# An attention-and-gate kernel on one core: small tiled matmuls made full-array, and the start-up reordered

## The chip, the cores and the metric

The kernel runs on one core of a Trainium2 chip. The metric is device time in microseconds (us), lower is better; "before" means the kernel as it was, "the change" or "after" the changed one. The profile's span runs from the first to the last instruction of one profiled execution and is 1 to 2 us shorter than the measured time. Engines: PE is TensorE, PEld its weight loads, DVE is VectorE, ACT is ScalarE, POOL is GpSimd, SP only issues DMAs here. Every run has a state (fast or slow); only fast runs are compared, and where a profile fell in the slow state the text says so.

## The reference

Eight batches, eight heads, 576 positions, head size 64. Attention is approximated with 32 landmarks, the means of 18 positions each:

```python
q_lm = q.reshape(B, H, 32, 18, D).mean(axis=3);  k_lm = ...      # landmarks
A, Bm, C = sm(q, k_lm), sm(q_lm, k_lm), sm(q_lm, k)              # softmax of scaled products
Z = Bm^T / (norm1(Bm) * norminf(Bm))
for _ in range(6): Z = 2*Z - Z @ Bm @ Z                          # Newton, 32 x 32 per head
x = A @ Z @ C @ v
# then the gate, on x laid out as (batch, 576, 512)
proj = x @ w_proj;  x1, x2, x3 = split(proj)
y = x1 * irfft(rfft(x2) * rfft(filter)) * x3                     # over the 576 positions
out = y @ w_out
```

## The kernel before

Each batch has an attention part and a gate part. The gate of batch b is interleaved ("woven"), step by step, with the second half of the attention of b+1 and the first half of b+2. Each engine runs its own list of instructions in order, so a step that waits on TensorE's list holds up all steps behind it (in the changed kernel below TensorE stands 6.7 us for one turned K, with other work behind it in its list). FFTs are matmuls with tables of cosines and sines. Scores need K and Q with the head dimension on partitions; K and Q are loaded in natural layout by GpSimd's queue and *turned*: batch 0 by TensorE, batches 1 to 7 by a DMA transpose on SP's queue. SP's queue also carries the output stores.

```python
    def load(b, by_dma=True, with_v=True):
        kn = io.tile([R, H, NC, D], BF16, tag="kn", name="kn")      # two buffers
        qn = io.tile([R, H, NC, D], BF16, tag="qn", name="qn")
        nc.gpsimd.dma_start(kn..., k[b]...)
        nc.gpsimd.dma_start(qn..., q[b]...)
        if with_v: load_v(b)
        if by_dma:                                                   # the DMA turns
            for src, dst in ((kn, kTbufs[b % 2]), (qn, qTbufs[b % 2])):
                nc.sync.dma_start_transpose(dst[:, 0:NB, :], src...)
    ...
        def newton(last):                       # 32 x 32 tiles, 8 heads as 2 x 4
            for g in range(2):
                for a in range(4):
                    o = slice(32 * a, 32 * a + 32)
                    mm(pn[o, 1, g, :], i32[o], RZ[o, 1, g, :], start=True, stop=False)
                for a in range(4):
                    o = slice(32 * a, 32 * a + 32)
                    mm(pn[o, lo:2, g, :], RZ[o, 0, g, :], RZ[o, lo:2, g, :], start=False, stop=True)
    ...
        def scores(T, e, x, t):                 # one burst; six of them in a batch
            for h in range(H):
                for o in (0, 64):
                    mm(pc[:, o // 64, sl * m:(sl + 1) * m], Tf[o:o + 64, lo:lo + P], lm[o:o + 64, t, h, :])
            nc.scalar.activation(e[:, 2 * x:2 * x + 2, :], pc[:R, :, 0:256], AF.Exp, ...)
    ...
    # main
    tables_fwd(kc, nrow); tables_inv(sc, kb)
    for s in att[0][0] + att[0][1]: s()         # attention of batch 0
    load(1); ...; filter_spectrum(); load(2)
    for s in att[1][0]: s()                     # first half of batch 1, before gate 0
    for b in range(B):
        if b + 3 < B: load(b + 3, with_v=False)
        side = att[b + 1][1] + [load_v(b + 3)] + att[b + 2][0]      # (shortened)
        _weave(gate(b, res[b]), side)
```

The softmax here doesn't subtract the row's maximum and nothing guards it: scores larger than these inputs give would overflow.

Of the kernel before, what the change touches and what calls it, by code (L numbers as in the profile page):

```python
# [15 lines left out]
PI = math.pi  # L16
# [17 lines left out]
def kernel(  # L34
# [22 lines left out]
    FW = 2 * P + 3 * QR  # L57
# [29 lines left out]
    loaded = {}  # L87
# [6 lines left out]
    def load(b, by_dma=True, with_v=True):  # L94
        kn = io.tile([R, H, NC, D], BF16, tag="kn", name="kn")
        qn = io.tile([R, H, NC, D], BF16, tag="qn", name="qn")
        vn = vbufs[b % NV]
        nc.gpsimd.dma_start(kn.rearrange("p h c d -> p h (c d)"),
                            k[b].rearrange("h (p c) d -> p h (c d)", c=NC))
        nc.gpsimd.dma_start(qn.rearrange("p h (e c) d -> p (h e) (c d)", e=2),  # L100
                            q[b].rearrange("h (e p c) d -> p (h e) (c d)", e=2, c=3))
        if with_v:
            load_v(b)
        if by_dma:
            for src, dst in ((kn, kTbufs[b % 2]), (qn, qTbufs[b % 2])):
                nc.sync.dma_start_transpose(dst[:, 0:NB, :],
                                            src.rearrange("p h c d -> p (h c d)"))
        loaded[b] = (kn, qn, vn)

    load(0, by_dma=False)  # L110
    wproj = consts.tile([P, 4, 3 * Dm], BF16, name="wproj")
    wsrc = moe_w_proj.rearrange("(c p) j -> p c j", p=P)
    for jb in (1, 0, 2):
        nc.gpsimd.dma_start(wproj[:, :, Dm * jb:Dm * (jb + 1)],
                            wsrc[:, :, Dm * jb:Dm * (jb + 1)])
        if jb == 1:
            filt = big.tile([R, 2, 3, Dm], BF16, tag="G", name="filt")
            nc.gpsimd.dma_start(
                filt.rearrange("p e c j -> p e (c j)"),
                moe_filter_fft.rearrange("(e p c) j -> p e (c j)", e=2, c=3))  # L120
# [6 lines left out]

    poolk = consts.tile([R, m], BF16, name="poolk")
# [11 lines left out]
    nc.vector.tensor_copy(identh, ident)  # L140
    dup = consts.tile([P, 2, D], F16, name="dup")
# [25 lines left out]
    def attention(b, res, first=False):  # L167
# [3 lines left out]
        def begin():  # L171
            kn, qn, vn = loaded.pop(b)
            st.update(kn=kn, qn=qn, vn=vn, pl=wtile())
# [48 lines left out]
        def landmarks():  # L222
# [6 lines left out]
            for par in range(2):  # L229
# [3 lines left out]
            nc.vector.tensor_scalar(lm.rearrange("p t h l -> p (t h l)"), pl3,  # L233
                                    1.0 / blk, None, op0=ALU.mult)
# [3 lines left out]
        def b_scores():  # L238
# [19 lines left out]
            st.update(Bn=Bn, BT=BT)  # L258

        def b_residual():  # L260
            Bn, BT = st["Bn"], st["BT"]
            psC = stile()
            mm(psC[:, 64:128], blk4.rearrange("p a l -> p (a l)"),
               Bn.rearrange("p g l -> p (g l)"))
            for g in range(2):
                for a in range(4):
                    o = slice(32 * a, 32 * a + 32)
                    mm(psC[o, 32 * g:32 * g + 32], BT[o, g, :], BT[o, g, :])
            cm = sm.tile([P, 2], F32, tag="cm", name="cm")
            nc.vector.tensor_reduce(cm, psC[:, 64:128].rearrange("p (g l) -> p g l", g=2),  # L270
# [3 lines left out]
            RZ = sm.tile([P, 2, 2, m], F16, tag="RZ", name="RZ", bufs=3)  # L274
            for g in range(2):
                nc.vector.scalar_tensor_tensor(
                    RZ[:, 0, g, :], in0=psC[:, 32 * g:32 * g + 32],
                    scalar=cm[:, g:g + 1], in1=i32, op0=ALU.mult, op1=ALU.add)
            nc.vector.scalar_tensor_tensor(
                RZ[:, 1], in0=Bn, scalar=-1.0,  # L280
# [3 lines left out]
        steps.append(b_scores)  # L284

        def newton(last):

            RZ = st["RZ"]
            pn = stile()[:, 0:128].rearrange("p (t g l) -> p t g l", t=2, g=2)
            lo = 1 if last else 0  # L290
            for g in range(2):
                for a in range(4):
                    o = slice(32 * a, 32 * a + 32)
                    mm(pn[o, 1, g, :], i32[o], RZ[o, 1, g, :], start=True, stop=False)
                for a in range(4):
                    o = slice(32 * a, 32 * a + 32)
                    mm(pn[o, lo:2, g, :], RZ[o, 0, g, :], RZ[o, lo:2, g, :],
                       start=False, stop=True)
            if last:
                Zb = sm.tile([P, 2, 4, m], F16, tag="Zb", name="Zb")  # L300
                nc.vector.tensor_tensor(
                    Zb, pn[:, 1].unsqueeze(2).to_broadcast([P, 2, 4, m]),
                    blk4.unsqueeze(1).to_broadcast([P, 2, 4, m]), op=ALU.mult)
                st["Zb"] = Zb
            else:
                nx = sm.tile([P, 2, 2, m], F16, tag="RZ", name="RZ", bufs=3)
                nc.scalar.copy(nx, pn)  # L307
                st["RZ"] = nx

        def scores(T, e, x, t):  # L310
            pc = wtile()
            lm = st["lm"]
            Tf = T.rearrange("p x r -> p (x r)")
            for h in range(H):
                g = h // 4
                sl = 4 * g + ((h % 4) ^ g)
                lo = (3 * h + x) * R
                for o in (0, 64):
                    mm(pc[:, o // 64, sl * m:(sl + 1) * m],
                       Tf[o:o + 64, lo:lo + P], lm[o:o + 64, t, h, :])  # L320
            nc.scalar.activation(e[:, 2 * x:2 * x + 2, :], pc[:R, :, 0:256],  # L321
                                 AF.Exp, bias=0.0, scale=scale)

        def c_scores(x):
            if x == 0:
                st["eC"] = big.tile([R, NC, 256], BF16, tag="eC", name="eC", bufs=1)
            scores(kTbufs[b % 2], st["eC"], x, 1)

        def a_scores(x):
            if x == 0:  # L330
                st["eA"] = big.tile([R, NC, 256], BF16, tag="eA", name="eA", bufs=1)
            scores(qTbufs[b % 2], st["eA"], x, 0)

        steps.append(lambda: c_scores(0))
        steps.append(b_residual)
        steps.append(lambda: c_scores(1))
        steps.append(lambda: newton(False))
        steps.append(lambda: c_scores(2))
        steps.append(lambda: newton(False))
        steps.append(lambda: a_scores(0))  # L340
        steps.append(lambda: newton(False))
        steps.append(lambda: a_scores(1))
        steps.append(lambda: newton(False))
        steps.append(lambda: a_scores(2))
        steps.append(lambda: newton(False))

        def cv():
# [3 lines left out]
            for g in range(2):  # L351
                for c in range(NC):
                    for a in range(4):
# [11 lines left out]
            Cv = sm.tile([P, 2, D], BF16, tag="Cv", name="Cv")  # L365
            nc.vector.tensor_tensor(Cv, p3[:, :, 0:D],
                                    rC.unsqueeze(2).to_broadcast([P, 2, D]),
                                    op=ALU.mult)
# [22 lines left out]
        def zcv():  # L391
            pz = stile()
            for g in range(2):
                for o in (0, 64):
                    mm(pz[o:o + 64, 128 * g:128 * g + 128], st["Cv"][:, g, :],
                       st["Zb"][:, g].rearrange("p a l -> p (a l)"))
# [28 lines left out]
    INV = consts.tile([P, 5, HS], F16, name="INV")  # L425
    HH = consts.tile([P, 2, 2, 2, Dm], BF16, name="HH")
    HE = consts.tile([P, 2, 256], BF16, name="HE")
    wk = consts.tile([P, 1], F32, name="wk")
    half_pi = consts.tile([P, 1], F32, name="half_pi")
    lohi = consts.tile([P, 2], F32, name="lohi")  # L430
    TS = 2.0 * PI / S * (1.0 - 1e-7)

    def iota(t, pattern, base, cm):
        nc.gpsimd.iota(t, pattern=pattern, base=base, channel_multiplier=cm,
                       allow_small_or_imprecise_dtypes=True)
# [20 lines left out]
    def tables_iota():  # L456
        nc.vector.memset(half_pi, PI / 2)
        kc = consts.tile([R, 2 * Q + 1], F32, name="kc")
        iota(kc[:, 0:2 * Q].rearrange("p (e r) -> p e r", e=2), [[1, 2], [2, Q]], 0, 0)
        nc.vector.memset(kc[:, 2 * Q:2 * Q + 1], float(HS))  # L460
        nrow = consts.tile([R, 3], F32, name="nrow")
        iota(nrow, [[1, 3]], 0, 3)
        sc = consts.tile([P, HS], F32, name="sc")
        iota(sc, [[1, 3], [3, R]], 0, 0)


        kb = consts.tile([P, 3], F32, name="kb")
        iota(kb[:, 0:2], [[1, 2]], 0, 2)
        iota(kb[:, 2:3], [[0, 1]], 0, 1)
        return kc, nrow, sc, kb  # L470

    def tables_fwd(kc, nrow):
# [7 lines left out]
        for src, fn, tt in ((w, cosine, 0), (t, minus_sine, 1)):  # L480
            s4 = src[:, :, 0:2 * Q].rearrange("p c (e r) -> p c e r", e=2)
            for c in range(3):
                fn(F[:, c, :, P * tt:P * tt + P], s4[:, c, :, 0:P])
            lo = 2 * P + QR * tt
            for c in range(3):
                fn(F[:, c, :, lo:lo + QR], s4[:, c, :, P:Q])
        cosine(F[:, :, 0, P:P + 1], w[:, :, 2 * Q:n])
        nc.gpsimd.tensor_copy(F[:, :, :, 2 * P + 2 * QR:FW],
                              F[:, :, :, 2 * P:2 * P + QR])

    def tables_inv(sc, kb):


        x = consts.tile([P, 4], F32, name="xr")
        for a in range(4):
            o = slice(32 * a, 32 * a + 32)
            nc.vector.tensor_scalar(x[o, 0:1], kb[o, 2:3], -32.0 * a, None, op0=ALU.add)
            nc.vector.memset(x[o, 2:3], 256.0 + a % 2)
        nc.vector.tensor_scalar(lohi[:, 1:2], x[:, 0:1], 16.0, None, op0=ALU.is_ge)
# [11 lines left out]
                                op0=ALU.mult)  # L511
        nc.vector.memset(wk, 2.0 / S)
# [11 lines left out]
        sine(INV[:, 4, :], t[:, 2, :])  # L524
# [6 lines left out]
    def filter_spectrum():  # L531
        fs = big.tile([R, 2, 3, Dm], F16, tag="Y", name="fs")
        nc.vector.tensor_tensor(fs[:, 0], filt[:, 0], filt[:, 1], op=ALU.add)
# [201 lines left out]
    for s in att[1][0]:  # L735
        s()
# [41 lines left out]
```

## Time and profile before

The start of the first forward matmul of a batch's gate (`w<-F,AE` in the timeline) is used as that batch's mark throughout. A *stretch* is the time from one mark to the next; in the steady state it is the *period*.

| | before |
|---|---|
| measured, median | 274.07 us |
| first mark, second mark | 55.7, 88.7 us |
| period | 26.89 us |
| last two stretches (gate 6, gate 7 to the end) | 18.4, 30.5 us |

From the page of the kernel before, the forty-slice lines of TensorE, its granted clock and the DMA engines; each digit is a slice of 6.8 us, in tenths:

```profile
PE   0401569789999899989998999999998999998880
...
PEclk9999999999999999999999999999999999999997
DMA  6999999999999999689998997990240024006005
```

TensorE is busy from the seventh slice on, and the DMA engines are nearly full for the first 27 slices, that is 184 us. From the list of waits, the first 56 us (who waited for whom, total us, times, longest):

```profile
DVE fs L533 <- DMA filt<-in_moe_filter_fft_dram: 16.9, 1, 16.9
...
PE s L203 <- DVE kT_74 L207: 14.9, 1, 14.9
```

VectorE stood 16.9 us for the filter's load, because the filter sums came first in its list; TensorE's turn of batch 0 then stood 14.9 us for a VectorE copy behind them. The stretches of the kernel before (columns: from and to, length, busy us and count of PE, PEld, DVE, ACT, POOL, granted clock, DMA share, GB/s):

```profile
0.00:55.70 55.70, 25.57 (x572) 16.89 (x572) 26.56 (x93) 22.03 (x45) 18.04 (x47) 1.00 1.27 175
55.70:88.70 33.00, 31.39 (x549) 17.43 (x544) 20.68 (x49) 20.00 (x38) 2.52 (x3) 1.00 1.43 156
88.70:115.60 26.90, 25.82 (x476) 15.01 (x464) 19.56 (x44) 18.50 (x35) 2.51 (x3) 1.00 1.07 175
```

The trace's clock records begin only at 66.9 us, and where there is none the profile shows 1.00.

TensorE is busy 25.8 of 26.9 us in a period, but matmuls are pipelined (one of 288 columns is drawn as some 290 ns long, and the next starts 122 ns after it), so this overstates it. Start-to-start times say more: in a steady run a matmul of 288 columns follows the last one after 122 ns, one of 512 columns after 216 ns. The Trainium skill, page "TensorE: Matmul & The Clock Gate", section "Back-to-back issue gap", gives columns / 2.4 + 2.5 ns as the gap of a single matmul on the warm array, 122.5 and 215.8, and the trace agrees; the shorter gap that it gives for a sustained stream, some 131 ns at 512 columns, does not show here: 80 such gaps in four periods have a median of 216 ns, and none is under 215. Whatever a start-to-start time has above that (by over 30 ns) is called a pause here. A period then has 20.3 us of streaming, 3.9 us in 41 pauses whose releaser is "issue", and 2.7 us of waits for other engines. Where those 95 ns pauses stand is seen in the timeline of PE, merged, columns start, length, instruction:

```profile
158.29 0.34 PE L77 MATMUL w<-lm,kT_77 64*128 64x32 bf16 x13
158.56 0.30 PE L77 MATMUL w<-INV,Y 128*128 128x288 f16 x1
158.79 0.22 PE L77 MATMUL s<-BT 32*32 32x32 f16 x8
158.94 0.54 PE L77 MATMUL w<-INV,Y 128*128 128x288 f16 x3
```

One 288-column matmul starts at 158.56 and the next burst, of 32 by 32 tiles, at 158.79: 230 ns, of which 122 are streaming.

### The profile page before, as it was taken

To read this page: it belongs to the slowest core of one execution; us is meant where nothing else is said; L and a number is where in the kernel's file an instruction comes from. 1 tells how busy PE (TensorE), PEld (TensorE's weight loads), DVE (VectorE), ACT (ScalarE), POOL (GpSimd) and SP (SyncE) were. 2 spreads that over 40 slices of the span, in tenths; PEclk is the share of its full clock that TensorE was granted. 3 is DMA by queue.
4 is the path that set the end of the run, shared out by engine and by line. 5 is a ranking of instruction groups with operands and counts; after the bars stand their busy time and mean duration, and the time that the engine had idled before them with its cause. 6 is when DMAs were issued, how large, how long until landed. Compare 5 with 4: busy or idle time off the path is not lost.

```text
span 272.3 us, 8683 instructions
## 1 busy us (share of the span) xinstructions
PE 224.8 (83%) x3796; PEld 127.5 (47%) x3796; DVE 173.9 (64%) x417; ACT 161.0 (59%) x288; POOL 28.9 (11%) x60
## 2 busy tenths in 40 slices
PE   0401569789999899989998999999998999998880
PEld 0401435444654466446644664566445544633430
DVE  1029766482883878388838883798379838952950
ACT  1102974465665676667766776676667668539530
POOL 8910201201200120012001200100000000000000
PEclk9999999999999999999999999999999999999997
DMA  6999999999999999689998997990240024006005
GB/s 86 199 209 202 194 172 157 175 154 155 181 128 163 201 185 202 117 179 140 138 160 158 215 143 117 181 127 2 59 120 2 2 64 116 0 0 176 0 4 171
DMA packets 66422, 35.10 MB, mean 129 GB/s; under 512 B 46736, under 2 KB 62096, under 8 KB 66384
## 3 DMA queue, kind: packets, MB, share of 16 engines
q0 software_dynamic: 27280, 16.84, 48.3%
q1 hardware_dynamic: 39104, 17.70, 38.1%
q8 instruction: 29, 0.48, 0.8%
q14 instruction: 9, 0.07, 0.1%
HBM read 33.69 MB, written 9.44 MB: 158 GB/s over the span
## 4 chain that ended last, share of the span: by engine, by line
PE 56%; DVE 18%; ACT 13%; DMA 5%; issue 4%; POOL 1%; ACTq 0%; DVEq 0%; POOLq 0%
PE w L77 45%; PE s L77 9%; DMA filt<-in_moe_filter_fft_dram 5%; ACT X L607 4%; DVE rA L377 3%; PE s L414 2%; DVE T L609 2%; DVE gt L646 2%; DVE lm L233 1%; ACT G L598 1%; ACT eA L321 1%; ACT os L680 1%; DVE Y L611 1%; DVE rA L380 1%; DVE t L442 1%
## 5 line engine op out<-in xcount | busy, mean ns | idle before, releaser
L77 PE MATMUL w<-AT,G 128*128 128x288 f16 x256 | 41.0, 286 | 0.8 <-ACT x_5470 L644 0.4
L609 DVE TENSOR_TENSOR T<-X,HH 128x2048 bf16<-128x2048 bf16 x16 | 19.6, 1224 | 22.9 <-ACT X L607 22.9
L77 PE MATMUL w<-wout,y 128*128 128x512 bf16 x128 | 32.8, 381 | 0.4 <-DVE y L667 0.2
L377 DVE TENSOR_REDUCE rA<-eA 96x48 f32<-96x1536 bf16 x8 | 14.0, 1749 | 26.8 <-ACT eA L321 26.8
L77 PEld LDWEIGHTS <-G 128*128 128x128 bf16 x256 | 22.2, 97 | 11.3 <-issue 3.8
L598 ACT CAST G<-w 128x1024 bf16<-128x1024 f32 x24 | 24.5, 1020 | 3.6 <-PE w L77 3.6
L680 ACT COPY os<-w 128x1024 f32<-128x1024 f32 x16 | 16.2, 1012 | 16.5 <-PE w L77 16.4
L77 PE MATMUL w<-INV,Y 128*128 128x288 f16 x128 | 22.5, 288 | 0.4 <-ACT x_5443 L644 0.3
L77 PEld LDWEIGHTS <-y 128*128 128x128 bf16 (+1 forms) x192 | 13.8, 101 | 18.5 <-DVE y L667 5.4
L203 PE MATMUL s<-ident,kn 96*128 96x96 bf16 x24 | 2.4, 276 | 22.9 <-DVE kT_74 L207 14.9
L663 ACT COPY uo<-w 128x288 f32<-128x288 f32 x32 | 12.8, 399 | 13.1 <-PE w L77 9.4
L77 PE MATMUL w<-F,AE 96*128 96x304 f16 x96 | 18.9, 315 | 0.3 <-ACT os L680 0.3
L77 PE MATMUL w<-G,Ah 128*128 128x512 bf16 x64 | 18.2, 394 | 1.2 <-ACT G L598 0.5
L664 DVE TENSOR_TENSOR cv<-w,uo 128x288 bf16<-128x288 f32 x32 | 14.6, 455 | 6.7 <-ACT uo L663 6.0
L607 ACT CAST X<-w 128x1024 bf16<-128x1024 f32 x16 | 16.2, 1015 | 3.5 <-PE w L77 3.5
L587 ACT CAST Ah<-w 128x608 f16<-128x608 f32 x16 | 10.7, 671 | 11.3 <-PE w L77 11.3
L321 ACT ACTIVATE eA<-w 96x512 bf16<-96x512 f32 x24 | 13.9, 594 | 5.0 <-PE w L77 4.8
L321 ACT ACTIVATE eC<-w 96x512 bf16<-96x512 f32 x24 | 13.8, 593 | 3.8 <-PE w L77 3.1
L667 DVE TENSOR_TENSOR y<-cv,gt 128x576 bf16<-128x576 bf16 x32 | 14.5, 454 | 0.5
L665 DVE TENSOR_TENSOR cv<-w,uo 128x288 bf16<-128x288 f32 x32 | 14.3, 447 | 0.0
L307 ACT CAST RZ<-s 128x128 f16<-128x128 f32 x40 | 10.6, 266 | 5.9 <-PE s L77 5.2
L224 ACT CAST lmp<-w 128x768 f16<-128x768 f32 x8 | 6.5, 810 | 11.8 <-PE w L77 11.8
(236 smaller groups left out, 428.0 us busy)
## 6 DMA issues: line engine op xcount, KB each, us to landing
kn<-in_k_dram POOLq DMA_DIRECT2D x8, 576.0 KB, 11.5
qn<-in_q_dram POOLq DMA_DIRECT2D x8, 576.0 KB, 14.8
out_dram<-os SPq DMA_DIRECT2D x24, 192.0 KB, 3.0
vb_73<-in_v_dram POOLq DMA_DIRECT2D x4, 576.0 KB, 9.6
vb_76<-in_v_dram POOLq DMA_DIRECT2D x4, 576.0 KB, 9.2
out_dram<-os SPq DMA_DIRECT2D x16, 128.0 KB, 2.4
wproj<-in_moe_w_proj_dram POOLq DMA_DIRECT2D x3, 512.0 KB, 15.9
out_dram<-os SPq DMA_DIRECT2D x24, 64.0 KB, 2.5
```

Of the source, the lines that this page charges most:

```text
L77: nc.tensor.matmul(out_, lhsT, rhs, start=start, stop=stop, skip_group_check=True)
L321: nc.scalar.activation(e[:, 2 * x:2 * x + 2, :], pc[:R, :, 0:256], AF.Exp, bias=0.0, scale=scale)
L377: nc.vector.tensor_reduce(rA, eA.rearrange("p c (h l) -> p (c h) l", l=m), axis=AX.X, op=ALU.add)
L587: nc.scalar.copy(st["Ah"][:, g], pf[:, :, 0:FW])
L598: nc.scalar.copy(st["G"][:, :, Dm * jb:Dm * (jb + 1)], pg)
L607: nc.scalar.copy(X, px)
L609: nc.vector.tensor_tensor(T, X.unsqueeze(2).to_broadcast([P, 2, 2, Dm]), HH[:, f], op=ALU.mult)
L663: nc.scalar.copy(uo, pi[:, 1, 0:HS])
L664: nc.vector.tensor_tensor(cv_[:, 0, :], pi[:, 0, 0:HS], uo, op=ALU.add)
L665: nc.vector.tensor_tensor(cv_[:, 1, :], pi[:, 0, 0:HS], uo, op=ALU.subtract)
L667: nc.vector.tensor_tensor(st["y"][:, j, :].rearrange("p (e s) -> p e s", e=2), cv_, st.pop(f"gt{j}"), op=ALU.mult)
L680: nc.scalar.copy(os, po)
```

## The change

Its intent: (1) Newton, the residual before it, ZCv and the rest frequencies of the FFT as matmuls over the full 128 by 128 array, with block-diagonal operands, so that TensorE changes its tiling less often; (2) scores in three bursts instead of six; (3) the index tables ahead of the loads, the filter sums behind batch 0's landmarks, batch 1's first half woven into gate 0 instead of standing before it; (4) the loads of batch 2 held until batch 1 is turned. The diff, cut to its core:

```diff
+    load_k(0)                       # after the first iotas, not before everything
...
     def load_k(b):
         kn = io.tile(...)
+        ins = nc.gpsimd.dma_start(kn..., k[b]...)
+        if b == 2:
+            tc.add_manual_dep(ins.ins, after[1].ins.name, DependencyInfo(Sync, DATA))
...
+    def turn_kq(b):
+        for src, dst in zip(loaded[b], (kTbufs[b % 2], qTbufs[b % 2])):
+            after[b] = nc.sync.dma_start_transpose(dst[:, 0:NB, :], src...)
...
+            BTd = sm.tile([P, 2, 4, m], F16, ...)      # B transposed, block-diagonal
+            nc.vector.tensor_tensor(BTd, BT..., blk4..., op=ALU.mult)
...
         def newton(last):
-            pn = stile()[:, 0:128]...
+            pn = stile()[:, 0:320].rearrange("p (g x) -> p g x", g=2)
+            mm(pn[:, :, P:160], identh, RZ[:, :, P:160], start=True, stop=False)
             for g in range(2):
-                ... 16 matmuls of 32 x 32 tiles
+                mm(pn[:, g, lo:160], RZ[:, g, 0:P], RZ[:, g, lo:160], start=False)
...
+        steps.append(c_scores)          # two slots of K in one burst, one wide exp
+        steps.append(b_residual)
+        steps.append(lambda: newton(False))
+        steps.append(rest_scores)       # last slots of K and Q in one burst
+        steps.append(lambda: newton(False))
+        steps.append(a_scores)
...
         def spectrum_rest():
-            ... 16 matmuls of 32-column tiles, two products, one sum
+            for g in range(2):
+                mm(px, st["AhE"][:, g]..., st["G"][:, g, Dm:2 * Dm], start=(g == 0), stop=(g == 1))
+            nc.vector.tensor_tensor(YE, X, HE, op=ALU.mult)
...
             for f in range(2):                          # inverse of the rest
-                mm(pi[:, f, 0:HS], st["YE"][o, ...], INV[o, 4, :], ...)            # 32 rows
+                mm(pi[:, f, 0:HS], st["YE"][:, P * j:P * j + P], INV[:, 4 + f, :], ...)   # 128 rows
...
     for b in range(B):
+        side = []
+        if b == 0: side += att[1][0]
         if b + 3 < B:
-            load(b + 3, with_v=False)
-        side = []
+            side.append(lambda b=b: load_kq(b + 3))     # now a step of the weave
```

## The prediction

> **What bounds it now.** Three stretches, read from the timeline and the per-stretch table. (1) Start-up: the first forward matmul of batch 0 starts at 55.7 us. VectorE took the filter sums first and stood 16.9 us for the filter's load (list of waits); the tables, and the copies that free PSUM for TensorE's turns, came behind it, so TensorE's turn of batch 0 waited 14.9 us, landmarks came at 31.3 us. All of batch 1's first half then also ran before batch 0's gate. (2) Steady state: a batch every 26.89 us. TensorE bounds it, in order: from start-to-start times of one period I get 20.3 us of streaming, 3.9 us in 41 pauses of about 95 ns whose releaser is "issue", and 2.7 us of waits for VectorE or ScalarE. VectorE is busy 19.6, ScalarE 18.5 us. (3) Tail: 18.4 + 30.6 us. Beside this the DMA engines are at 0.9 or more from 7 to 184 us (forty-slice line): a second bound close behind.
>
> The Trainium skill, "TensorEngine Tiling (Array Packing)", Key Properties, says that changing the tiling mode drains TensorE. The trace agrees: the 95 ns pauses stand where the shape changes between full array and 32- or 64-row or -column tiles.
>
> **What the change does, per batch.** Newton, B residual, ZCv, rest spectrum and rest inverse become full-array; scores go from six bursts to three. About 25 tiled bursts become about 9: some 25 drains x 95 ns = -2.4 us. Streaming: Newton 1.4 to 0.9 us, rest spectrum 0.76 to 0.43 (two 512-wide at 216 ns), ZCv -0.1; but rest inverse loses its pairing, 0.5 to 1.0, and forward widens, +0.1. Net -0.4 us. ScalarE: five Newton copies grow from 266 to about 430 ns (+0.8), exps save 0.4, forward copies 0.15. VectorE: +0.8 us (rest-frequency copy, block-diagonal B, wider Cv and residual), -0.3 in the rest product. Neither becomes the bound, but VectorE reaches about 83% and the waits grow some 0.3 us. Period: 24.5 us.
>
> **Start-up.** Index tables ahead of loads and filter sums behind the landmarks remove the VectorE stall: landmarks near 15 us, forward of batch 0 near 28 us instead of 55.7. Batch 1's first half is woven into gate 0, so that stretch grows from 33.0 to about 35 us although the drains shrink. Holding batch 2's loads lets batch 1's two transposes (18 us each beside loads) finish near 39 us instead of 51. Second forward: 63 us instead of 88.7.
>
> **Sum.** 63 + 5 x 24.5 + 17.3 + 30 = 233 span, about +1 to the measured time, +2 for DMA collisions: 236 us. DMA check (estimate): from 39 us, 18 loads of 2.95 us, 12 transposes of about 4.4 us and five outputs of 6 us need 139 us, so batch 7 is turned by about 180 to 187 us, just when compute wants it. Nearly all start-up gain is on the critical path, unless DMA catches it.
>
> Prediction 236 us, 8 in 10 within 228 to 246. Faster by over 2%: 0.97, within: 0.02, slower: 0.01.
>
> **Right if:** no filter wait before landmarks; forward of batch 0 at 25 to 32 us; steady spacing of forwards 24 to 25.3 us; "issue" pauses 14 to 20 per batch. **Wrong if:** gates 0 to 2 wait for DMA (waits of TensorE on turned K or Q, spacing over 27 us early), meaning DMA became the bound and the total nears 245; the Newton chain, now with longer copies and three rounds in a row, puts a wait on ScalarE; or ScalarE's table switches hold up batch 0's exps.

## The result

The change runs in 256.67 us, median of 4 runs (254.32 to 256.95), against 274.07 us before. The ratio is 0.9351, 95% interval 0.9274 to 0.9429. A ratio here is the mean time of one kernel's fast runs over that of the other's in the same rounds, so not quite the ratio of the medians. The prediction of 236 us, range 228 to 246, was wrong: of some 38 us of forecast gain 17 came.

| us | before | predicted | after |
|---|---|---|---|
| first mark | 55.7 | 28 | 32.2 |
| first stretch | 33.0 | 35 | 48.6 |
| second mark | 88.7 | 63 | 80.8 |
| second stretch | 26.9 | 24.5 | 26.5 |
| period | 26.89 | 24.5 | 25.17 |

The forty-slice lines of the change (slices of 6.4 us):

```profile
PE   0377980898369998999899989998999999999980
...
PEclk9999997599859999999999999999999999999995
DMA  5999999999999999999999899920240032015005
```

TensorE now starts early, but falls back in the seventh and the eleventh slice (0 and 3 tenths) and its clock sinks just after. (Here the clock records begin at 27.9 us; before that, start-to-start times of 426 ns at 512 columns say half clock.) The stretches after:

```profile
0.00:32.20 32.20, 17.76 (x289) 11.59 (x290) 25.96 (x92) 18.25 (x28) 16.46 (x42) 1.00 1.18 176
32.20:80.80 48.60, 32.70 (x571) 20.34 (x566) 25.72 (x65) 22.90 (x40) 5.77 (x7) 0.82 1.32 175
80.80:107.30 26.50, 24.65 (x369) 15.22 (x368) 23.23 (x50) 19.41 (x33) 2.51 (x3) 1.00 1.31 175
107.30:132.50 25.20, 23.87 (x367) 15.10 (x366) 20.51 (x47) 18.59 (x32) 2.51 (x3) 1.00 1.24 207
```

In the first stretch TensorE is busy 32.7 of 48.6 us, at 0.82 of its clock. What it waited for, from the list of waits of that stretch:

```profile
PE w L77 <- DMA kT_77<-kn: 6.7, 1, 6.7
...
PE w L77 <- DMA kT_74<-kn: 5.1, 1, 5.1
```

kT_77 is here the turned K of batch 1, kT_74 that of batch 2. Finer windows around the two waits (same columns):

```profile
38.00:44.80 6.80, 0.19 (x8) 0.08 (x8) 1.34 (x6) 0.71 (x2) 0.00 (x0) 0.76 1.45 129
44.80:51.80 7.00, 6.47 (x124) 3.13 (x125) 2.41 (x7) 4.96 (x7) 3.26 (x4) 0.50 1.09 178
66.90:72.10 5.20, 0.07 (x10) 0.02 (x4) 1.83 (x8) 0.22 (x1) 0.00 (x0) 0.68 1.31 183
72.10:75.70 3.60, 3.60 (x44) 1.99 (x44) 0.95 (x4) 1.42 (x2) 1.75 (x2) 0.51 1.26 156
```

Each wait is followed by some time at half clock: 7.0 us after the first, 3.6 us after the second. The wide matmuls' start-to-start times there are 1.8 to 2.0 times the warm ones. The Trainium skill, "TensorE: Matmul & The Clock Gate", Part 1, says that a window of about 3.4 us of idleness puts the array back to half rate. At the first wait this trace agrees: the clock falls 3.3 us after the last matmul (38.2 to 41.5 us). At the second it falls after only 1.9 us (66.9 to 68.8 us), with a few matmuls in the 1.5 us before. So a wait costs more than its length: 11.8 us of waits, and at most half of 10.6 us at half clock, that is up to 5 us more (an upper estimate, as not all of that time is bound by the array).

The chain of waits that ended last, in order of time (start, length, what), names the cause. It is the part from 10 to 75 us:

```profile
10.77 18.05 DMA kn<-in_k_dram
28.84 6.10 SPq L124
35.00 12.07 DMA qT_78<-qn
47.11 0.50 issue
47.63 7.54 DMA kn<-in_k_dram
55.18 16.85 DMA kT_74<-kn
72.08 2.16 PE w L77 x30
```

Read downwards: batch 1's K load, the issue of its K turn, its Q turn, then the held load of batch 2's K, its turn (16.9 us), and only then TensorE. For 60 us the critical chain is DMA work.

### The profile page after: what moved, and what is told of

Its sections match the earlier page's. It is cut to its first block, busy times and chain, and to the rows that moved or that the text cites. A ratio compares the mean times of both kernels' runs of the same rounds, so it can differ in the third digit from the quotient of the medians.

```text
span 255.0 us, 7085 instructions
## 1 busy us (share of the span) xinstructions
PE 208.8 (82%) x2996; PEld 127.3 (50%) x2996; DVE 183.2 (72%) x443; ACT 161.3 (63%) x266; POOL 30.5 (12%) x59
## 4 chain that ended last, share of the span: by engine, by line
PE 44%; DMA 21%; ACT 11%; DVE 11%; POOL 3%; issue 3%; SPq 2%; ACTq 0%; POOLq 0%
PE w L77 35%; DMA kn<-in_k_dram 10%; PE s L77 8%; DMA kT_74<-kn 7%; DMA qT_78<-qn 5%; SPq L124 2%; DVE cv L695 2%; ACT uo L694 2%; DVE gt L678 2%; ACT X L647 2%; ACT G L638 1%; ACT lmp L264 1%; ACT RZ L347 1%; DVE y L698 1%; PE s L465 1%
## 5 line engine op out<-in xcount | busy, mean ns | idle before, releaser
L77 PE MATMUL w<-wout,y 128*128 128x512 bf16 x128 | 32.2, 386 | 0.2
L77 PEld LDWEIGHTS <-G 128*128 128x128 bf16 x256 | 22.8, 97 | 12.2 <-issue 3.5
L77 PEld LDWEIGHTS <-y 128*128 128x128 bf16 (+1 forms) x192 | 14.6, 102 | 15.8 <-issue 2.5
L347 ACT CAST RZ<-s 128x320 f16<-128x320 f32 x40 | 17.3, 432 | 6.4 <-PE s L77 5.8
L77 PE MATMUL w<-F,AE 96*128 96x320 f16 x96 | 17.2, 300 | 0.3 <-ACT os L711 0.3
L366 ACT ACTIVATE eC<-w 96x1024 bf16<-96x1024 f32 x8 | 8.2, 1019 | 14.1 <-PE w L77 14.1
L625 DVE CAST AhE<-w 128x128 f16<-128x128 f32 x16 | 4.6, 290 | 16.0 <-ACT Ah L624 16.0
L77 PEld LDWEIGHTS <-Y 128*128 128x128 bf16 x128 | 11.1, 98 | 7.0 <-issue 3.5
L77 PE MATMUL s<-RZ 128*128 128x160 f16 (+1 forms) x96 | 14.0, 227 | 0.0
L103 POOL DMA_DIRECT2D kn<-in_k_dram x8 | 6.4, 804 | 62.5 <-DMA qT_78<-qn 28.8
```

The costliest lines, as they stand in the source:

```text
L77: nc.tensor.matmul(out_, lhsT, rhs, start=start, stop=stop, skip_group_check=True)
L347: nc.scalar.copy(nx, pn)
L366: nc.scalar.activation(e[:, 0:4, :].rearrange("p (x e) l -> p x e l", e=2), pc[:R].rearrange("p e (x l) -> p x e l", x=2), AF.Exp, bias=0. ...
```

## The experiments

Seventeen kernels ran. All gave results that passed the comparison with the reference, also the one that is wrong. The table has their marks from the profiles; "DMA turns" counts the DMA transposes issued. "Mean" is over the fast runs, whose number is given. The 95% intervals reach 0.003 to 0.014 to either side of the ratios.

| run | DMA turns | 1st, 2nd, 3rd, 4th mark (us) | mean of fast runs | ratio to before |
|---|---|---|---|---|
| before | 14 | 55.7, 88.7, 115.6, 142.5 | 274 (median) | 1 |
| after | 14 | 32.2, 80.8, 107.3, 132.5 | 256.2 (4) | 0.935 |
| e1_no_hold | 14 | 31.4, 84.3, 110.7, 135.9 | 259.5 (4) | 0.945 |
| e2_hold_both | 14 | 31.5, 85.2, 111.6, 136.8 | 261.2 (4) | 0.950 |
| e9_hold3 | 14 | 31.3, 80.1, 106.6, 131.8 | 257.3 (4) | 0.938 |
| e10_hold3_both | 14 | profile in the slow state | 258.9 (2) | 0.945 |
| e11_need_order | 14 | 32.2, 72.6, 99.1, 134.8 | 260.5 (5) | 0.953 |
| e14_order23 | 14 | 31.9, 72.7, 107.9, 136.2 | 258.8 (4) | 0.941 |
| e5_arrays_only | 14 | 52.2, 84.3, 109.0, 133.8 | 255.7 (2) | 0.931 |
| e6_start_only | 14 | 33.3, 83.7, 110.5, 137.0 | 268.2 (2) | 0.977 |
| e13_newton_tiled | 14 | 35.4, 80.4, 107.5, 135.8 | 261.7 (4) | 0.955 |
| e16_front | 14 | 32.5, 80.1, 106.0, 130.7 | 254.1 (4) | 0.926 |
| e3_pe_turn1 | 12 | 32.1, 69.8, 101.0, 126.1 | 252.3 (3) | 0.919 |
| e8_turn1_hold3 | 12 | profile in the slow state | 247.7 (2) | 0.902 |
| e12_turn1_order | 12 | profile in the slow state | 248.3 (2) | 0.906 |
| e15_turn1_hold34 | 12 | 32.6, 74.4, 100.9, 126.0 | 251.7 (4) | 0.915 |
| e4_pe_turn12 | 10 | 31.4, 70.0, 97.4, 122.6 | 247.9 (2) | 0.902 |
| e17_turn12_front | 10 | 31.1, 71.3, 98.1, 122.8 | 246.9 (4) | 0.900 |
| e7_no_turn | 0 | 31.6, 67.0, 93.4, 118.6 | 241.7 (4) | 0.880 |

For e5_arrays_only (two of its four runs were slow) 0.931 is worked out from its two fast runs and the five fast runs of before.

### Is it the hold? (e1_no_hold)

```diff
-        if b == 2:
+        if b == -2:          # never
             tc.add_manual_dep(ins.ins, after[1].ins.name, ...)
```

> The changed kernel without the hold on batch 2's K load. Hold theory (the hold put load of K2, its turn and batch 1's turns in series, so that batch 0's gate stands for K2 and its turned copy): the turned K of batch 2 lands near 58 us instead of 72.0, the stretch from the first forward of batch 0 to that of batch 1 falls from 48.6 to about 41 us, total near 248 us. DMA-capacity theory (the engines are full whatever the order): the stretch stays 47 to 50 us and the total 254 to 258 us.

The hold theory fell. The turned K of batch 2 did land earlier, at 63.0 us, but its Q only at 77.2 us, the first stretch grew to 52.9 us and the time was 259.2 us (median). The hold in the change is neutral or a little good.

### The two halves of the change apart (e5_arrays_only, e6_start_only)

e5 is the kernel before with the hunks of the diff that change matmuls, tables and bursts; e6 is the kernel before with the hunks that change loads, their order, the filter sums and the main loop.

> The kernel before with only the full-array matmuls and score bursts; loads, tables and order of batches as before. If the parts are independent: period 25.2 us, second forward near 87.5 us (before 88.7), total near 262 us. If the start-up order also made the shorter period possible: period above 26 us and total above 266 us.

> The kernel before with only the new order of loads, tables, filter sums and batch 1's first half, and the hold; tiled matmuls as before. If the parts are independent: first forward near 32 us, second near 82 us, period 26.9 us, total near 266 us. If the start-up's DMA waits hide the array gain in the first stretch: second forward as in the full change (80.8), total near 265 us as well; above 268 us would say the start-up change alone is worth little.

The array part alone reaches 255.7 us in fast runs, as much as the full change (256.2). Its stretches:

```profile
0.00:52.20 52.20, 23.16 (x480) 15.24 (x480) 27.81 (x106) 21.30 (x34) 17.43 (x46) 0.99 1.25 177
52.20:84.30 32.10, 29.79 (x384) 17.35 (x378) 25.81 (x57) 20.79 (x36) 2.85 (x4) 0.85 1.41 164
84.30:109.00 24.70, 23.83 (x366) 15.21 (x364) 19.03 (x44) 18.71 (x32) 2.51 (x3) 1.00 1.30 197
```

Its first mark is 20 us later than that of the full change and its second mark only 3.5 us later. In its first stretch TensorE waits only 1.5 us for a DMA (the turned Q), where the full change waits some 12: it comes late enough to find batch 2 nearly turned. Alone, the start-up part is worth 2.3% (0.977, interval 0.969 to 0.985); e6's first mark is 33.3 us, as expected, and its second 83.7 us.

One thing that the halves were not built to show: in all 15 profiles of kernels with both the new start-up and full-array Newton the full clock comes at 26.3 to 29.4 us; in the two with the new start-up and tiled Newton (e6, and e13 below) only at 50.0 and 55.1 us. So e6 runs its first gate at half clock for 16.7 us. Why is not tested.

### Amount of DMA work, or compute? (e3_pe_turn1, e7_no_turn, e4_pe_turn12)

e3 and e4 let TensorE turn batch 1, or 1 and 2, as it does batch 0, and drop the hold:

```diff
-        turn_kq(b)
+        if b >= 2:           # e4: 3
+            turn_kq(b)
...
-        if first:
+        if by_pe:            # b < 2, e4: b < 3
             for n in range(3):
                 steps.append(lambda n=n: turn(st["kn"], kTbufs[b % 2], n))
```

e7 drops all DMA turns and scores every batch against batch 0's turned K and Q. That is wrong; it still passes the comparison, as Q, K and V are a tenth of normal random numbers and the softmaxes nearly flat: with this edit in the reference, the outputs of batches 1 to 7 change by about 0.1%.

```diff
-        turn_kq(b)
-            both(kTbufs[b % 2], st["eC"], 1)
+            both(kTbufs[0], st["eC"], 1)        # and likewise for Q
```

> No hold, and batch 1's K and Q turned by TensorE as batch 0's are, so no scores of batch 1 wait for a DMA transpose. DMA-wait theory: the 6.7 us wait for the turned K of batch 1 goes, batch 2 is turned about 9 us earlier, the first stretch is about 36 us, total near 243 us. Rival (the first stretch is long because it carries one more half batch of compute, DMA waits only fill time that VectorE and ScalarE need anyway): the extra turns and copies make it no shorter than without the hold, total 248 us or more.

> Wrong result on purpose: no DMA turn at all, every batch scores against batch 0's turned K and Q; no hold (there is nothing to hold for). Loads and outputs stay. DMA-capacity theory (until the second or third gate the loads and turns together ask more of the DMA engines than they can give, so the gates end when batch 2 and 3 are turned): the first stretch falls from 48.6 to 35-38 us, the second to 25-26, total 236 to 243 us, that is the predicted time. Rival (compute in the first gate, with its extra half batch and waits for VectorE and ScalarE): first stretch stays above 43 us, total above 250 us.

> No hold; batches 0, 1 and 2 turned by TensorE, batches 3 to 7 by DMA. DMA-capacity theory: with four DMA turns fewer before gate 2, first stretch 38 us (one more set of turns on TensorE), second stretch 26 to 28 us instead of the 31.2 us of the kernel that turns only batch 1 so; total 244 to 248 us. Rival (order, not capacity): second stretch stays 30 us or more, total 250 us or more.

e7 behaves as the DMA theory says. Its stretches:

```profile
0.00:31.60 31.60, 17.48 (x291) 11.56 (x292) 25.59 (x93) 18.25 (x28) 17.67 (x44) 1.00 1.18 175
31.60:67.00 35.40, 31.17 (x570) 19.78 (x567) 25.24 (x65) 22.62 (x40) 4.38 (x6) 0.95 1.13 160
67.00:93.40 26.40, 24.55 (x369) 15.17 (x367) 23.20 (x50) 19.34 (x33) 2.52 (x3) 1.00 0.69 112
```

The first stretch is 35.4 us (predicted for the change: 35), the DMA share in the second stretch falls from 1.31 to 0.69, and the total is 241.6 us. So the change has 13 us there that go with the DMA turns: the waits for them and the half clock after. The compute of the stretch came out as predicted, but partly by luck: the 33.0 us from which the prediction started had 11.2 us at half clock, e7's 35.4 have 3.4 us, and the difference (an estimate: up to half of 7.8 us) was not in the sum. e3 removes the wait of the first stretch (37.7 us), but its second stretch is 31.2 us: the wait moved on by a batch. e4 goes one batch further: 38.6, then 27.4 us, then the undisturbed 25.15 us.

### Or their order? (e9_hold3, e10_hold3_both, e11_need_order, e2_hold_both, e14_order23)

A load that is not needed yet shares the engines with the turn that is needed next. These runs add holds to the change: loads of batch b wait for the turns of batch b-1.

```diff
-        if b == 2:
-            tc.add_manual_dep(ins.ins, after[1].ins.name, ...)     # after[1] is the Q turn
+        if b in (2, 3):                    # e11: (2, 3, 4)
+            wait_turns(ins, b - 1)         # both turns; in e11 and e14 for K and for Q
```

e9 and e10 hold K of batch 2 and K and Q of 3, e9 behind the Q turn alone; e2 holds K and Q of batch 2 only.

> The changed kernel with one more hold: K and Q of batch 3 wait until batch 2 is turned. Order theory: the turn of batch 2's K takes about 6 us instead of 16.9, lands near 61 us instead of 72, second forward near 71 to 74 us instead of 80.8, total near 249 us. Capacity theory: batch 3 comes later by as much as batch 2 comes earlier; third forward stays near 107 us, total 255 to 258 us.

> The changed kernel with K and Q of batch 3 held behind both turns of batch 2 (the run with one hold more tied them to the Q turn alone, which the queue took first, so K2's turn still shared the engines). Order theory: K2's turn takes about 6 us and lands near 61 us, second forward 70 to 74 us, third 97 to 101, total 247 to 251 us. Capacity theory: second forward earlier, third forward unchanged near 106 us, total 255 to 257 us.

> The changed kernel with K and Q of batches 2, 3 and 4 all held behind both turns of the batch before (in the changed kernel only K of batch 2 is held; its Q is issued at 17.8 us and shares the engines with K1's turn). Order theory: K1 turned near 37 us instead of 44.8, K2 near 54, second forward 66 to 70 us, third 92 to 96, total 243 to 247 us. Capacity theory: idle engines during the holds cost what the order gains; total 252 us or more.

> The changed kernel with Q of batch 2 held as well as K. K1 is turned near 41 us instead of 44.8 (so TensorE waits 3.4 us for it instead of 6.7), but K2's turn still shares the engines with batch 3's loads: second forward 77 to 79 us instead of 80.8, total 253 to 255 us. If Q2's early load costs nothing: total 256 to 258 us.

> The changed kernel with K and Q of batches 2 and 3 held behind both turns of the batch before, batch 4 free. Order theory: second forward near 72.6 us and third near 99 us as in the run that held batch 4 too, then no stall in the third stretch (25.2 us instead of 35.7), total 247 to 250 us. If amount decides: the lost time comes back in the third or fourth stretch (over 28 us), total 255 us or more.

e9 tested nothing new: the queue took batch 2's Q turn before its K turn, so the hold was released before the turn that it should protect. In e10, e11 and e14 order works where it acts: in e10 (a slow run, so only the single DMA is read) the K turn of batch 2 took 7.1 us instead of 16.9; in e11 and e14 the second mark came 8 us earlier. But no order was faster than the change; the wait moved. In e14 it stands in the second stretch, in e2 in the first, on the turned Q this time (lists of waits, e14 from 72 to 108 us, then e2 from 31 to 85 us):

```profile
PE w L77 <- DMA qT<-qn: 7.4, 1, 7.4
```

```profile
PE w L77 <- DMA qT<-qn: 9.0, 2, 8.5
PE w L77 <- DMA kT<-kn: 5.0, 2, 3.2
```

In e11 it took another form. The stores of the outputs stand behind the turns in SP's list, and the next turn waited for a held load, so the output buffers did not come free; ScalarE stood for a store and TensorE for ScalarE (list of waits of e11, 99 to 135 us):

```profile
ACT os L718 <- DMA out_dram<-os: 8.3, 1, 8.3
...
PE s L77 <- ACT RZ L354: 7.7, 1, 7.7
```

The fourth mark sums it up. With the same matmuls (but for TensorE's own turns) and 14 DMA turns it lies between 131.8 and 136.8 us in every fast profile, whatever the order (the change, e1, e2, e9, e11, e14); with 12 turns at 126 (e3, e15), with 10 at 122.6 (e4), with none at 118.6 (e7). This speaks for the amount of DMA work, but does not prove it. A turn on TensorE takes away the traffic and also the chain of load, then turn, that a batch has to wait for, and no run separates the two. And order counts for something: e12 below, in its profile (of a slow run), has its fourth mark at 121.3 us with 12 turns and loses the time later, in stretches of 26.8 and 30.5 us. Whether a still better order exists, with stores and turns kept from blocking each other, is left open.

### Amount and order together (e8_turn1_hold3, e12_turn1_order, e15_turn1_hold34)

All three turn batch 1 on TensorE and hold the loads of batch 3, of 3 to 6, or of 3 and 4.

> Batch 1 turned by TensorE, and K and Q of batch 3 not loaded before batch 2 is turned. Order theory (loads ahead of their need share the engines with the turn that is needed next): batch 2's two turns take about 6 us each instead of 17 and 20, first stretch about 36 us, and batch 3 is turned by 80 us, second stretch 27 us, total near 245 us. Capacity theory: batch 2 comes earlier but batch 3 just as late (87 us), the sum of the first two stretches stays 67 to 70 us, total 250 to 254 us.

> Batch 1 turned by TensorE, K and Q of batches 3 to 6 held behind both turns of the batch before: less DMA work and in the order of need. Both theories together: no TensorE wait for DMA after 32 us, stretches 36.5, 25.5 and 25.2 us, total 242 to 245 us, the best of all.

> Batch 1 turned by TensorE; K and Q of batches 3 and 4 held behind both turns of the batch before, 5 and 6 free (the run with those held too had stretches of 26.8 and 30.5 us behind blocked stores). Expected stretches 37.9, 26.5 and then 25.2 us each, total 242 to 245 us, best of all; if the stall only moves, 248 us or more.

None reached what was expected of it (near 245, or 242 to 245 us); the means of the fast runs are 247.7, 248.3 and 251.7 us. In e15 all stretches after the first are free of DMA waits (26.5, then 25.17 us), but the first is 41.7 us, with the clock at half from 33 to 47 us without a long wait before (the longest in the 14 us before was 2.3 us):

```profile
26.00:33.00 7.00, 5.54 (x83) 2.98 (x81) 5.56 (x14) 4.20 (x7) 0.00 (x0) 1.00 1.44 199
33.00:46.60 13.60, 12.96 (x158) 9.04 (x157) 5.58 (x13) 4.60 (x7) 0.77 (x1) 0.50 1.37 178
```

The last but two of these columns is the granted clock, 0.50 in the second window. These versions are not better than e4, which uses no hold. Against e3, which has the same turns and no hold (252.3 us), e8 and e12 are about 4 us faster in the mean of two fast runs each; the intervals overlap, so this is not shown.

### The period (e13_newton_tiled, e16_front)

e13 is the change with Newton and the residual as 32 by 32 tiles, as before. e16 moves one line back:

```diff
-        if b + 3 < B:
+        if b + 3 < B and b:
+            load_kq(b + 3)                  # ahead of the weave, as before
+        elif b == 0:
             side.append(lambda b=b: load_kq(b + 3))
```

> The changed kernel with Newton and the B residual as 32 by 32 tiles again. Drain theory: 12 more issue pauses a batch of 95 ns (+1.1 us), streaming 0.2 us less; period 25.9 to 26.2 us instead of 25.16, and 0 to 2 us more in total than six such steps, as the first stretch waits for DMA anyway: total 260 to 263 us. Rival (streaming count is what matters): period about 25.0 us, total 256 us.

> The changed kernel, with the loads of batch b+3 issued ahead of the weave instead of as its first step, for b of 1 and more. If the place of the woven steps makes the difference: period 24.74 us, total about 254 to 255.5 us (5 periods x 0.42 us less). If the loads' later issue in time is not the cause and the place is not either: period 25.16 us, total 256 to 258 us.

e13's period is 25.43 us: both theories missed, and full-array Newton is worth 0.27 us of a period, not the 0.9 that 12 drains less 0.2 us of streaming make. Its trace settles why, once three missing records of 512-column matmuls in a period are put back (each leaves a gap 216 ns too long): 20.4 us of streaming, 1.9 us in 21 pauses, 3.1 us of waits. That is 0.2 us less streaming than the change, as expected, but 6 pauses more and not 12. The others stand inside a wait for another engine, or beside another tiled burst, where a pause stays in either form. The total is 5.5 us longer, and most of this is outside the steady state: first mark 3.1 us later, third stretch 28.3 us instead of 25.2. The clock has a part in both: it is at half up to 55.1 us (27.9 in the change) and for 3.4 us of that third stretch. e16 has a period of 24.74 us, as expected, and 254.0 us: making the issue of loads a step of the weave cost 0.42 us a period in waits. The run moves both the issue of the loads and the place of every woven step behind it; e7, where the DMA engines have much less to do (share 0.73 in its third stretch), has the period of the change, 25.16 us, which speaks for the place.

### The best version (e17_turn12_front)

e4 with e16's line.

> Batches 1 and 2 turned by TensorE, no hold, loads ahead of the weave: the gains add to stretches of 38.6, 27 and then 24.74 us, total 245 to 247 us, the best; if they do not add, as before 247 to 251 us.

It ran in 246.78 us (median; 246.48 to 247.70), ratio 0.9002, 95% interval 0.8964 to 0.9039: the fastest correct kernel, 3.7% below the change by the ratios. Its stretches:

```profile
31.10:71.30 40.20, 35.03 (x655) 24.55 (x652) 31.82 (x79) 22.21 (x38) 5.03 (x6) 0.96 1.27 173
71.30:98.10 26.80, 25.75 (x385) 15.97 (x380) 23.10 (x50) 20.59 (x35) 2.51 (x3) 1.00 1.22 170
98.10:122.80 24.70, 23.83 (x366) 15.20 (x365) 20.39 (x47) 18.70 (x32) 2.51 (x3) 1.00 1.12 181
```

## Why the prediction was wrong

The predicted span was 233 us, the measured one 255.0, 22 us more. Term by term:

1. **The first stretch, predicted 35 us, measured 48.6 (13.6 us of the miss).** The step that failed is the DMA check: "from 39 us, 18 loads of 2.95 us, 12 transposes of about 4.4 us and five outputs of 6 us need 139 us, so batch 7 is turned by about 180 to 187 us". It summed the work up to the *last* batch and found room there, and there was room: batch 7 was turned at 159.0 us. The shortage was at the *first* batches: starting TensorE 23 us earlier brought forward when batches 1 and 2 are needed, and the engines, full from the start, could not follow. Three parts of it were wrong in size: a turn at "about 4.4 us" (no turn of the kernel before took less than 5.3 us, and those of batches 1 and 2 took 10 to 18), "batch 1's two transposes ... finish near 39 us" (measured 44.8 and 47.1, as the Q load of batch 2 was not held and shared the engines; in e2, which holds it, 40.6 and 42.6), and nothing was allowed for batch 3's loads beside batch 2's K turn. The prediction named the danger ("gates 0 to 2 wait for DMA") and put the total at 245 us in that case; it came out nearly 12 us above even that. With no DMA turns at all the stretch is 35.4 us: its compute came out right, partly by luck, as said above.
2. **The first mark, predicted 28 us, measured 32.2.** The filter wait is gone, as predicted. But landmarks came at 19.2 us, not 15: TensorE's turns waited 4.0 us in all for VectorE's copies, which still had the tables before them. No run tests whether this is the cause.
3. **The period, predicted 24.5 us, measured 25.17; over the five stretches that the sum counts with it, 126.3 us instead of 122.5.** From the start-to-start times (two periods each):

| us in a period | before | predicted | after | only arrays |
|---|---|---|---|---|
| streaming | 20.3 | 19.9 | 20.6 | 20.6 |
| pauses by issue (number) | 3.9 (41) | 1.5 (16) | 1.4 (15) | 1.4 (15) |
| waits for other engines | 2.7 | 3.0 | 3.2 | 2.7 |
| period | 26.89 | 24.5 | 25.17 | 24.74 |

   The drains went as predicted. The failed term is streaming, "Newton 1.4 to 0.9 us, rest spectrum 0.76 to 0.43": the 1.4 and the 0.76 had the drains in them, which were then subtracted a second time. Without them Newton streams 0.78 us before and 0.92 after, so block-diagonal operands cost streaming rather than save it, and the rest inverse lost its pairing as predicted (0.5 to 1.0 us). The waits grew by 0.5 us, of which e16 gives back 0.4: the shifted weave, not foreseen.
4. **The tail** (predicted 47.3, measured 47.8 us) was right.

So the array part gave 7%, nearly all of the result, and the start-up part, of which the prediction expected some 25 us, gave nothing on top of it: TensorE's early start was paid back at the turns of batches 1 and 2, in waits of 12 us and in half clock after each.

What stays open: whether the orders tried are near the best one for 14 DMA turns, how much of e4's gain is less traffic and how much the shorter chain, and why e15's clock fell without a long wait.

## What to carry to other kernels

When a start-up is moved forward, add up the DMA work *up to each early need*, not only to the end: engines that were nine tenths busy from the start had nothing to give here, and the earlier start turned into waits, made longer by the half clock behind them. Then reduce the amount (here, TensorE turns two batches in time that it would have waited) before refining the order. When pauses are costed as a term of their own, the durations beside them must be taken free of pauses; and the pauses that a change removes must be counted one by one, as a pause inside a wait or beside another tiled burst stays (6 vanished with Newton's tiles, not 12). And where a trace has no clock record, the start-to-start times of wide matmuls tell the clock.

## What the Trainium skill lacked or had wrong

- "TensorEngine Tiling (Array Packing)", Key Properties, says that a change of tiling mode drains TensorE, but not what it costs. Here a switch showed as a pause of about 95 ns, 41 times a period before and 15 after; taking Newton's tiles away removed 6 of them and shortened the period by only 0.27 us.
- "DMA: Bandwidth & Descriptors", section "Latency and other measured facts", gives 261 GB/s for a DMA transpose, measured on one kernel. Here the turn of batch 7's K, 590 KB with little other traffic beside it (0.74 MB in all), took 5.06 us from its issue to its landing (150.50 to 155.56 us), that is 117 GB/s; the shortest turn of the changed kernel took 4.9 us, and one beside loads 16.9 us.
- "TensorE: Matmul & The Clock Gate", Part 1, has the return to half clock after an idle window of about 3.4 us; the runs agree in part (0.50 of the clock for 7.0 us after a wait of 6.7 us, but also a fall after 1.9 us without a matmul). That many short idles can do the same is said there too, but not how much activity, or of which tiles, keeps the clock up: in e15 it fell at 33.1 us with TensorE busy 5.5 of the 7 us before, and with Newton tiled (e13) it came up at 55.1 us instead of 27.9.
